# LSH attention and two-layer network on one core: the products of the second layer regrouped by type, and one more raw weight buffer

## The chip, the cores and the metric

The kernel runs on one core of a Trainium2 chip. The metric is the device time of one execution in microseconds (us). The engines are TensorE (PE, with its weight loads shown apart as PEld), VectorE (DVE), ScalarE (ACT), GpSimd (POOL) and SyncE (SP), which here only issues transfers.

## What is computed

Attention over 4 batches of 8 heads, 768 positions and 64 dimensions, in which a query sees only the keys with the same 6-bit hash; then, on the 3072 tokens of 512 values that it gives, a network with a squared ReLU.

```python
q_bits = einsum(q, proj) > 0 ; k_bits = einsum(k, proj) > 0      # 6 bits each
scores = where(q_bucket == k_bucket, q @ k.T / 8, -1e9)
attn = softmax(scores) ; x = attn @ v                            # x: 3072 x 512
h = x @ w_in                                                     # w_in: 512 x 2048
g = s * max(h, 0)**2 + b
out = g @ w_out                                                  # w_out: 2048 x 512
```

## The kernel before, in words

Everything is unrolled, and the order of the work is made by a planner. Each piece of work is added to `Plan` with an engine, a cost in us, what it reads and writes, and a priority; `Plan.order` plays a list schedule with these costs and sorts the pieces by their planned start. Each engine then works through its own list in that order, and a piece on PE that waits holds all that stand behind it.

Attention goes through 96 slots (batch, head, third of the queries: 256 queries). A slot has score products (lines 621 and 622), a row maximum (626), an exponential (627), a normalization on GpSimd (646) and products with the values (686, or 692 and 698). When the last head of a batch is through, `moe` is called for each third of that batch: 256 tokens and 8 steps of two 128-wide slices of the 2048 hidden values, so 96 steps in all. Its PE work has the lowest priority and fills the places that attention leaves. The first batch is gone through in two passes over the hidden values, as its weights are decoded meanwhile.

A step of `moe` (names and lines as in the profile):
- first layer: 24 products with 256 columns of two fp16 planes of x and w_in (lines 794 to 796) into one PSUM bank (5);
- on ScalarE a ReLU out of the bank (804, tile `rb`, one buffer), the square (805), and s and b applied into `ghb`, in 4-byte form (fp32r, two buffers, 806);
- on GpSimd the same in full precision (807) and what `ghb` lost, as bf16, into `glb` (two buffers, 808). The planner counts 0.77 and 1.27 us for these two;
- second layer: 12 products with 512 columns (line 821), for each of two slices and two groups of 128 tokens three of them: z = 0 is `w` with `ghb`, both in 4-byte form; z = 1 is `wl`, the bf16 rest of w_out, with the upper halves of `ghb` read as bf16; z = 2 is `wp`, w_out as bf16, with `glb`. The token groups add up in PSUM banks 6 and 7.

The second layer comes in parts. With HALVES the first part holds z = 0 and z = 1, taken in turn for each slice and token group (eight products, waiting for `ghb`, `w`, `wl`), and the second part z = 2 (four products, waiting for `glb`). The very last step of the kernel takes all three in turn. The planner counts 0.2343 us for z = 0 and 0.2165 for each of the others. The second layer of a step stands behind the first layer of the following step by priority.

Weights come in 32 blocks, decoded by `decode` (lines 362 to 441) while the first 44 slots run: four w_in blocks and four w_out blocks make a group. A block's raw words are loaded from a transfer on ScalarE's queue (line 381) into one of NWR buffers, taken in turn. A w_out block leaves its buffer as soon as it is decoded. The four w_in blocks of a group hold theirs until their common scale is known (one transpose on PE, line 447, which takes its turn with the scales of the values) and they are split into two planes (433 to 438). A second rule lets at most two blocks be loaded ahead of decoding (`PACE`).

Of the kernel before, what the change touches and what calls it, by code (L numbers as in the profile page):

```python
# [168 lines left out]
def lsh_attention_moe(ctx: ExitStack, tc, q, k, v, proj, w_in, w_out, s, b, out):  # L169
# [26 lines left out]
    def f32(ap):  # L196
        return ap.bitcast(F32)

    def top(ap):

        return ap.bitcast(BF16).rearrange("p (n t) -> p n t", t=2)[:, :, 1]
# [8 lines left out]
    def pe(cost, fn, r, w, pr):  # L210
        plan.add(PE, cost, fn, r, w, pr)

    def dve(n, fn, r, w, pr, ns=None):
        plan.add(DVE, ((n + 64) / 960.0 if ns is None else ns), fn, r, w, pr)

    def act(n, fn, r, w, pr, more=0.0, late_=0.0):
        plan.add(ACT, 0.21 + n / 1470.0 + more, fn, r, w, pr, late_)

    def pool(n, fn, r, w, pr, ns=None):
        plan.add(POOL, (0.08 + n / 430.0 if ns is None else ns), fn, r, w, pr)  # L220

    def some(n, fn, r, w, pr, ways, slow=0.0):

        cost = {ACT: 0.21 + n / 1470.0, DVE: (n + 64) / 960.0, POOL: slow or 0.05 + n / 760.0}
        eng = {ACT: nc.scalar, DVE: nc.vector, POOL: nc.gpsimd}
        plan.any([(e, cost[e], lambda e=e: fn(eng[e])) for e in ways], r, w, pr)
# [135 lines left out]
    def decode(u, pr):  # L362
        src, key = dec[u]
        box = {}
        wi = key[0] == "wi"
        tag = f"wr{u % NWR}"

# [398 lines left out]
    def moe(bb, c, g0=0, g1=NF // 4):  # L766
# [15 lines left out]
        for f0 in range(fa, fz, 2):  # L782
            while nd[0] < f0 // 4 * 8 + 6 + f0 % 4:
                yield
            u = nu[0] % 2
            nu[0] += 1
            fill = 1e5 + 100.0 * nu[0]
            for j in range(2):
                hp, fs = bank[:, 5, j * CH:(j + 1) * CH], slice((f0 % 4 + j) * P, (f0 % 4 + j + 1) * P)
                for cc in range(NC_):  # L790
                    def mm(cc=cc, hp=hp, fs=fs, n=f0 // 4):
                        xc = boxes[cc][0]["t"][:, boxes[cc][1]]
                        w = wt[("wi", n, cc)]
                        nc.tensor.matmul(hp, w[:, 0, fs], xc[:, 0, :], start=(cc == 0), stop=False)  # L794
                        nc.tensor.matmul(hp, w[:, 1, fs], xc[:, 0, :], start=False, stop=False)  # L795
                        nc.tensor.matmul(hp, w[:, 0, fs], xc[:, 1, :], start=False, stop=(cc == NC_ - 1))  # L796
                    pe(0.327, mm, [boxes[cc][2], ("wi", f0 // 4, cc, 0), ("wi", f0 // 4, cc, 1)], [("b", 5)], fill)
            r, rk = rb, "r"
            gh, gl, hk, lk = ghb[:, u], glb[:, u], ("gh", u), ("gl", u)
            g4 = f0 // 4  # L800
            ds, dk = dsc[:, bb, g4:g4 + 1], ("ds", bb, g4)
            if c == 0 and f0 % 4 == 0:
                dve(1, lambda g4=g4, ds=ds: nc.vector.tensor_tensor(ds, vsc[:, bb, 1:2], wsc[:, g4, 1:2], ALU.mult), [("sc", bb), ("wsc", g4)], [dk], MP, 0.1)
            some(2 * CH, lambda e, r=r, ds=ds: e.activation(r, bank[:, 5, :], AF.Relu, scale=ds) if e is nc.scalar else e.tensor_scalar(r, bank[:, 5, :], ds, 0.0, ALU.mult, ALU.max), [("b", 5), dk], [rk], MP, (ACT, DVE))  # L804
            act(2 * CH, lambda r=r: nc.scalar.activation(r, r, AF.Square), [], [rk], MP)
            act(2 * CH, lambda r=r, gh=gh: nc.scalar.activation(gh, r, AF.Identity, bias=b_sb, scale=s_sb), [rk, "sb"], [hk], MP, 0.15)  # L806
            pool(2 * CH, lambda r=r: nc.gpsimd.tensor_scalar(r, r, s_sb, b_sb, ALU.mult, ALU.add), [hk, "sb"], [rk], MP, 0.77)  # L807
            pool(2 * CH, lambda r=r, gh=gh, gl=gl: nc.gpsimd.tensor_tensor(gl, r, f32(gh), ALU.subtract), [rk, hk], [lk], MP)  # L808

            end = bb == B - 1 and c == NCH - 1 and f0 == NF - 2  # L810
            for part in ((0, 1), (2,)) if HALVES and not end else ((0, 1, 2),):
                for jt in range(2 * TPC):
                    j, t = (jt % 2, jt // 2) if end else (jt // TPC, jt % TPC)
                    f = f0 + j

                    def mm2(f=f, j=j, t=t, gh=gh, gl=gl, part=part):
                        ts = slice(j * CH + t * P, j * CH + (t + 1) * P)
                        o = bank[:, 6 + t, :]
                        w = wt[("wo", f)]
                        for z in part:  # L820
                            nc.tensor.matmul(o, (gh, top(gh), gl)[z][:, ts], (w[0], w[1], w[2] if PLANE else top(w[0]))[z], start=(f == fa and z == 0), stop=(f == fz - 1 and z == 2))  # L821
                    ks_ = [[hk, ("wo", f, 0)], [("wo", f, 1)], [lk, ("wo", f, 2 if PLANE else 0)]]
                    pe(sum((0.2343, 0.2165, 0.2165)[z] for z in part), mm2, [k for z in part for k in ks_[z]] + [("wo", f, 0)], [("b", 6 + t)], fill + 150)
# [39 lines left out]
    for i in range(NSL):  # L863
        pr = 10.0 * i
        bb, h, c, w = slots[i]
        last = c == NCH - 1
        if last and w + 2 < len(visits):
            parts = prep(w + 2, i, pr)
        if c == h == 0 and bb + 1 < B:
            value_scale(bb + 1, pr + VLATE)  # L870
        weights(i, pr + WP)
        while nd[0] < min(ND, decodes(i)):
            decode(nd[0], pr + 15)
            nd[0] += 1
        now, parts = (parts, []) if not last else (parts[:2], parts[2:])
        values(i, pr + 5, now)
        for bb, h, c, w in [slots[x] for x in closed]:
            last = c == NCH - 1
            if last and w + 2 < len(visits):
                prep_values(w + 2, pr + 12)  # L880
            if h == H - 1:
                todo.append(moe(bb, c, 0, PASS if bb == 0 else NF // 4))
                if bb == 0 and last:
                    todo.extend(moe(bb, c2, PASS, NF // 4) for c2 in range(NCH))
        closed.clear()
        while todo and next(todo[0], True):
            todo.pop(0)
# [14 lines left out]
CONVCOST = 0.95  # L902
RATE = 1.0
PACE = 2
HALVES = True
DSTART = 3
NNAT = 2
NWR = 6
VLATE = 60
VZERO = 10  # L910
TOP = 2.0**15
# [43 lines left out]
```

## Time and profile before

| | us |
|---|---|
| median of 3 runs | 970.77 (969.79 to 971.96) |
| the profiled execution | 973.35 |
| its span, first to last instruction | 971.6 |
| PE busy in the span | 924.2 |
| VectorE, ScalarE, GpSimd busy | 625.5, 660.9, 624.1 |

The profile is of one execution. It gives each instruction's start and duration; matmuls overlap in it, so the cost of one in a row of them is read from the start of one to the start of the next. The granted clock of PE is given as a share of 2.4 GHz. Idle time is put down to what released the engine last; an engine that isn't the bottleneck loses nothing by it.

### The profile page before, as it was taken

To read this page: it belongs to the slowest core of one execution; us is meant where nothing else is said; L and a number is where in the kernel's file an instruction comes from. 1 tells how busy PE (TensorE), PEld (TensorE's weight loads), DVE (VectorE), ACT (ScalarE), POOL (GpSimd) and SP (SyncE) were. 2 spreads that over 40 slices of the span, in tenths; PEclk is the share of its full clock that TensorE was granted. 3 is DMA by queue.
4 is the path that set the end of the run, shared out by engine and by line. 5 is a ranking of instruction groups with operands and counts; after the bars stand their busy time and mean duration, and the time that the engine had idled before them with its cause. 6 is when DMAs were issued, how large, how long until landed. Compare 5 with 4: busy or idle time off the path is not lost.

```text
span 971.6 us, 18091 instructions
## 1 busy us (share of the span) xinstructions
PE 924.2 (95%) x6512; PEld 656.5 (68%) x6512; DVE 625.5 (64%) x1013; ACT 660.9 (68%) x1235; POOL 624.1 (64%) x714
## 2 busy tenths in 40 slices
PE   8999887899988999989999999999999999999997
PEld 5876665666655666757766776777777676666664
DVE  6688897777987676777777867667768775100000
ACT  3788776777767766767777787777687776434342
POOL 2467675768999656657757766676767676443433
PEclk7999989899999999989999999999999999999999
DMA  4376584565886978898899888797797776401000
GB/s 116 92 232 165 148 234 112 166 167 137 230 191 142 193 174 190 196 216 160 152 186 163 175 187 171 155 194 158 164 195 166 152 148 107 109 1 44 11 22 22
DMA packets 303721, 144.44 MB, mean 149 GB/s; under 512 B 264256, under 2 KB 286784, under 8 KB 303632
## 3 DMA queue, kind: packets, MB, share of 16 engines
q1 hardware_dynamic: 298432, 126.25, 60.3%
q10 hardware_dynamic: 5200, 17.05, 5.5%
q8 instruction: 51, 0.84, 0.4%
q14 instruction: 38, 0.31, 0.1%
HBM read 51.38 MB, written 14.16 MB: 67 GB/s over the span
## 4 chain that ended last, share of the span: by engine, by line
PE 56%; POOL 14%; issue 11%; DVE 10%; ACT 6%; DMA 2%; POOLq 0%; SPq 0%; ACTq 0%; DVEq 0%
PE bank L821 15%; PE bank L621 5%; PE bank L794 5%; PE bank L796 5%; PE bank L795 5%; PE bank L622 5%; PE bank L692 4%; POOL glb L808 4%; POOL eb L646 3%; POOL rb L807 3%; DVE st L626 3%; PE bank L686 3%; PE bank L678 3%; PE bank L698 2%; ACT eb L627 2%
## 5 line engine op out<-in xcount | busy, mean ns | idle before, releaser
L646 POOL TENSOR_SCALAR eb<-eb,st 128x768 f32<-128x768 f32 x176 | 194.2, 1110 | 50.3 <-DVE st L637 44.8
L794 PE MATMUL bank<-xc,wi 128*128 128x256 f16 x768 | 211.0, 275 | 1.4 <-ACT rb L804 1.3
L626 DVE TENSOR_REDUCE st<-bank 128x1 f32<-128x768 f32 x192 | 180.2, 952 | 47.0 <-PE bank L622 42.4
L795 PE MATMUL bank<-xc,wi 128*128 128x256 f16 x768 | 210.0, 273 | 0.0
L796 PE MATMUL bank<-xc,wi 128*128 128x256 f16 x768 | 209.9, 273 | 0.0
L627 ACT ACTIVATE eb<-bank,st 128x768 f32<-128x768 f32 x176 | 157.5, 896 | 66.0 <-DVE st L626 33.8
L807 POOL TENSOR_SCALAR rb<-rb,misc 128x512 f32<-128x512 f32 x96 | 84.7, 883 | 166.4 <-ACT ghb L806 164.6
L654 DVE SCALAR_TENSOR_TENSOR pb<-eb,pb 128x768 f16<-128x768 f32 x132 | 146.6, 1123 | 65.3 <-ACT pb L653 63.5
L821 PE MATMUL bank<-w,ghb 128*128 128x512 f32 x384 | 177.4, 534 | 0.0
L621 PE MATMUL bank<-ks,aq 128*128 128x384 f32 x384 | 156.5, 408 | 18.4 <-ACT eb L627 14.5
L804 ACT ACTIVATE rb<-bank,dsc 128x512 f32<-128x512 f32 x95 | 65.2, 687 | 144.2 <-PE bank L796 126.8
L821 PE MATMUL bank<-wl,ghb 128*128 128x512 bf16 x384 | 150.1, 391 | 0.0
L808 POOL TENSOR_TENSOR glb<-rb,ghb 128x512 bf16<-128x512 f32 x96 | 140.8, 1466 | 6.2
L622 PE MATMUL bank<-ks,bq 76*128 76x384 f32 x384 | 133.6, 348 | 1.1 <-DMA bq<-nat 1.1
L653 ACT ACTIVATE pb<-eb 128x768 f16<-128x768 f32 x132 | 108.2, 833 | 15.3 <-DMA tb<-pb 14.2
L821 PE MATMUL bank<-wp,glb 128*128 128x512 bf16 x384 | 102.7, 380 | 4.3 <-POOL glb L808 4.3
L621 PEld LDWEIGHTS bank<-ks,aq 128*128 128x128 f32 x384 | 75.7, 197 | 38.8 <-ACT eb L627 21.3
L821 PEld LDWEIGHTS <-ghb 128*128 128x128 bf16 x384 | 37.2, 97 | 86.6 <-issue 80.5
L794 PEld LDWEIGHTS <-wi 128*128 128x128 f16 x768 | 75.3, 98 | 30.1 <-issue 14.1
L795 PEld LDWEIGHTS <-wi 128*128 128x128 f16 x768 | 75.6, 98 | 19.4 <-issue 2.1
L631 POOL TENSOR_SCALAR st<-st 128x2 f32<-128x2 f32 x96 | 44.3, 462 | 66.5 <-DVE st L626 58.3
L844 DVE COPY osb<-bank 128x256 f32<-128x256 f32 x4 | 1.5, 420 | 127.4 <-PE bank L821 126.8
(141 smaller groups left out, 1656.2 us busy)
## 6 DMA issues: line engine op xcount, KB each, us to landing
ks<-aq SPq DMA_DIRECT2D x60, 192.0 KB
raw<-in_moe_w_in_dram ACTq DMA_DIRECT2D x16, 512.0 KB
raw<-in_moe_w_out_dram ACTq DMA_DIRECT2D x16, 512.0 KB
xc<-xd SPq DMA_DIRECT2D x60, 128.0 KB
nat<-in_q_dram SPq DMA_DIRECT2D x32, 192.0 KB
nat<-in_k_dram SPq DMA_DIRECT2D x32, 192.0 KB
vm<-in_v_dram SPq DMA_DIRECT2D x32, 192.0 KB
xd<-xsb SPq DMA_DIRECT2D x48, 128.0 KB
```

The source lines that it names most:

```text
L621: nc.tensor.matmul(o, aq[:, ts], ks[0][:, cols], start=True, stop=False)
L622: nc.tensor.matmul(o, bq[0:HR, ts], ks[1][0:HR, cols], start=False, stop=True)
L626: dve(S, lambda a=a, sc=sc: nc.vector.tensor_reduce(nm[:, a:a + 1], sc, AX.XY, ALU.max, negate=True), bk, [nk[a]], pr, 0.88)
L627: act(S, lambda a=a, sc=sc, e=e: nc.scalar.activation(e.rearrange("p (g n) -> p g n", g=2), sc, AF.Exp, bias=nm[:, a:a + 1], accum_out=z[: ...
L646: eng.tensor_scalar(e, e, rz[:, a:a + 1], u[:, a:a + 1], ALU.mult, ALU.add)
L654: dve(S, lambda e=e, hi=hi, lo=lo: nc.vector.scalar_tensor_tensor(lo, e, TOP, hi, ALU.mult, ALU.subtract), [ek, hk], [("lo", n)], pr, 1.0)
L794: nc.tensor.matmul(hp, w[:, 0, fs], xc[:, 0, :], start=(cc == 0), stop=False)
L795: nc.tensor.matmul(hp, w[:, 1, fs], xc[:, 0, :], start=False, stop=False)
L796: nc.tensor.matmul(hp, w[:, 0, fs], xc[:, 1, :], start=False, stop=(cc == NC_ - 1))
L807: pool(2 * CH, lambda r=r: nc.gpsimd.tensor_scalar(r, r, s_sb, b_sb, ALU.mult, ALU.add), [hk, "sb"], [rk], MP, 0.77)
L808: pool(2 * CH, lambda r=r, gh=gh, gl=gl: nc.gpsimd.tensor_tensor(gl, r, f32(gh), ALU.subtract), [rk, hk], [lk], MP)
L821: nc.tensor.matmul(o, (gh, top(gh), gl)[z][:, ts], (w[0], w[1], w[2] if PLANE else top(w[0]))[z], start=(f == fa and z == 0), stop=(f == f ...
```

## The change

The second layer's parts are now (z = 0) and (z = 1, z = 2): a step's four 4-byte products come first, waiting for `ghb` and `w`, and then eight bf16 products, waiting for `ghb`, `wl`, `wp` and `glb`. The last step of the kernel keeps all three in turn. NWR goes from 6 to 7: one more buffer of 4 KB a partition for raw weight blocks. The planner orders the whole program anew with both; no instruction is added or removed.

```diff
-            for part in ((0, 1), (2,)) if HALVES and not end else ((0, 1, 2),):
+            for part in PARTS if not end else ((0, 1, 2),):
...
-HALVES = True
+PARTS = ((0,), (1, 2))
...
-NWR = 6
+NWR = 7
```

## Rows read from the trace of the kernel before

**Rows 1.** The page: busy us (share) and instructions; chain that ended last; one group.
```profile
span 971.6 us, 18091 instructions
PE 924.2 (95%) x6512; PEld 656.5 (68%) x6512; DVE 625.5 (64%) x1013; ACT 660.9 (68%) x1235; POOL 624.1 (64%) x714
...
PE 56%; POOL 14%; issue 11%; DVE 10%; ACT 6%; DMA 2%; POOLq 0%; SPq 0%; ACTq 0%; DVEq 0%
...
L821 PE MATMUL bank<-w,ghb 128*128 128x512 f32 x384 | 177.4, 534 | 0.0
```

**Rows 2.** Stretches: length, busy us (instructions) by engine, granted PE clock, DMA share, GB/s.
```profile
250.00:300.00 50.00, 43.50 (x274) 28.62 (x272) 43.39 (x78) 35.09 (x62) 47.98 (x46) 1.00 0.78 183
350.00:415.00 65.00, 64.71 (x448) 45.03 (x447) 44.43 (x68) 46.05 (x82) 41.93 (x48) 1.00 0.87 189
415.00:440.00 25.00, 20.91 (x124) 13.94 (x121) 18.84 (x30) 15.51 (x30) 13.55 (x18) 0.86 0.91 207
440.00:500.00 60.00, 59.80 (x413) 42.29 (x413) 45.59 (x64) 43.05 (x77) 43.19 (x50) 1.00 0.86 161
...
845.00:960.00 115.00, 115.00 (x779) 76.93 (x777) 0.00 (x0) 48.33 (x71) 45.19 (x45) 1.00 0.05 18
```

**Rows 3.** Instruction groups from 440 us on: count, busy us, mean ns, idle before.
```profile
L821 PE MATMUL bank<-w,ghb 128*128 128x512 f32 x288 | 133.6, 539 | 0.0
...
L808 POOL TENSOR_TENSOR glb<-rb,ghb 128x512 bf16<-128x512 f32 x72 | 106.2, 1474 | 5.3
...
L807 POOL TENSOR_SCALAR rb<-rb,misc 128x512 f32<-128x512 f32 x72 | 58.4, 812 | 147.0 <-ACT ghb L806 146.8
```

**Rows 4.** Timeline of PE, one step in the tail: start us, duration us, instruction.
```profile
901.83 0.27 PE L795 MATMUL bank<-xc,wi 128*128 128x256 f16 x1
901.94 0.27 PE L796 MATMUL bank<-xc,wi 128*128 128x256 f16 x1
901.97 0.47 PE L821 MATMUL bank<-w,ghb 128*128 128x512 f32 x1
902.28 0.39 PE L821 MATMUL bank<-wl,ghb 128*128 128x512 bf16 x1
...
903.68 0.39 PE L821 MATMUL bank<-wl,ghb 128*128 128x512 bf16 x1
903.91 1.03 PE L821 MATMUL bank<-wp,glb 128*128 128x512 bf16 x4
904.78 0.27 PE L794 MATMUL bank<-xc,wi 128*128 128x256 f16 x1
```

**Rows 5.** Timeline of the weight loads in the same step.
```profile
902.75 0.10 PEld L821 LDWEIGHTS <-ghb 128*128 128x128 bf16 x1 [0.26 <-issue]
```

**Rows 6.** Timeline of PE where a second layer begins behind attention's 4-byte products.
```profile
729.26 0.39 PE L821 MATMUL bank<-w,ghb 128*128 128x512 f32 x1
729.49 0.39 PE L821 MATMUL bank<-wl,ghb 128*128 128x512 bf16 x1
```

**Rows 7.** Timeline of GpSimd and PE in the tail, the following step.
```profile
905.46 1.26 POOL L808 TENSOR_TENSOR glb<-rb,ghb 128x512 bf16<-128x512 f32 x1
...
907.32 0.47 PE L821 MATMUL bank<-w,ghb 128*128 128x512 f32 x1
```

**Rows 8.** PE's waits, 185 to 440 us (us, times, longest), and one of them.
```profile
PE bank L821 <- POOL glb L808: 2.9, 2, 1.8
...
276.70 1.26 POOL L808 TENSOR_TENSOR glb<-rb,ghb 128x512 bf16<-128x512 f32 x1
...
278.02 0.82 PE L821 MATMUL bank<-wp,glb 128*128 128x512 bf16 x3 [1.12 <-POOL glb L808]
```

**Rows 9.** Weight decoding: two raw loads as issued; VectorE's steps, ns min/median/max.
```profile
72.93 0.34 ACTq L381 DMA_DIRECT2D raw<-in_moe_w_out_dram  x1
...
109.25 0.34 ACTq L381 DMA_DIRECT2D raw<-in_moe_w_out_dram  x1
...
L396 DVE SCALAR_TENSOR_TENSOR raw<-osb,raw x32: 674/691/1540, 58.4 to 305.7; 128x512 int32<-128x512 int32 x32
```

## Prediction

> **What bounds the kernel now.** I read the page first, then the busy times by stretch, then single matmuls in order of time. The page gives TensorE (PE) 95% of the span and no other engine more than 68%, and PE has the largest share of the chain that ended last [rows 1]. A busy PE need not be PE at its peak, so I looked stage by stage [rows 2]. From 440 us on PE has no idle time to speak of (59.80 of 60 us at 440 to 500, 115.00 of 115 at 845 to 960) at the full granted clock, the 2.4 GHz level. Before that it waits: 43.50 of 50 us at 250 to 300, and 20.91 of 25 at 415 to 440, where the granted clock averages 0.86, so it stood at 1.2 GHz for part of the stretch, after waits for work. The reason lies in the order of work: the layers of a batch can start only when its last head is through attention. So there are two regimes. Up to about 440 us attention with its other engines sets the pace and PE time is worth little; from 440 us on the end is set by PE's own work, and each nanosecond taken out of it moves the end by about one.
>
> 72 of the 96 second-layer steps lie behind 440 us: of the 384 four-byte products [rows 1], four to a step, 288 start there [rows 3]. The last step keeps its old order by the code, so 71 count.
>
> **What regrouping the products removes.** One step of the tail shows the cadence, read from start to start [rows 4]. The last first-layer product starts at 901.94, the first bf16 product (wl) at 902.28: 0.34 less the 0.11 that a first-layer product takes (901.83 to 901.94) leaves 0.23 for the four-byte product (w) between them. From there to the fourth wl, 903.68, are three pairs in 1.40 us: 0.467 a pair. The fourth wl takes 0.23 (to 903.91), and the four wp products 0.87 (to 904.78): 0.2175 each. The step's twelve products take 2.73 us.
>
> So a bf16 product costs 0.2175 behind another of its kind, but 0.23 behind a four-byte one; that leaves 0.237 of a pair for a four-byte product behind a bf16 one. The weight loads give the reason for the first: the load for a wl product starts only at 902.75, when that product itself starts, having stood 0.26 us for "issue" [rows 5]; it isn't drawn ahead into the four-byte product.
>
> No 512-column four-byte product follows another in this trace, so the new cost of w is bounded. The nearest row is one that follows a four-byte product of attention, 384 columns wide: from 729.26 to 729.49, 0.23 us [rows 6]. I take 0.23, as it is the same instruction in the same neighbourhood. The lower end is a bf16 product's 0.2175, the upper end the 0.237 that it costs now.
>
> After the change a step has four w (0.23 each), one wl behind a four-byte product (0.23) and seven bf16 products behind bf16 ones (0.2175): 0.92 + 0.23 + 1.52 = 2.67 us, against 2.73: 0.06, or 0.057 with the terms unrounded. With w at 0.237 behind w only the three bf16 products gain, 3 x 0.0125 = 0.0375. With w at 0.2175 everywhere a step would take 2.61 and gain 0.12.
>
> 71 steps x 0.057 = 4.0 us, all in the stretch where PE is saturated (ends: 2.7 and 8.5). The 24 earlier steps save 1.4 us of PE time, but PE waits there and the next batch's start is attention's; between 0 and 1.4 I take 0.5, since only 350 to 415 us is nearly saturated (64.71 of 65) [rows 2].
>
> **What the regrouping adds: an earlier wait.** Four wl products that needed only ghb now stand behind the wait for glb (GpSimd), and behind them everything on PE, which is in order. So eight products need glb at 0.9 us into the step and not four at 1.9. In the tail the glb of a step ends at 905.46 + 1.26 = 906.72 and its first w starts at 907.32 [rows 7]; the first bf16 product would come at 908.24, so 1.5 us of slack cover it (2.5 now). I cost the wait at nothing there; the cover is the first layer of the following step, 24 products of 0.11, that stand ahead of it. If that cover were gone, up to 0.9 us of PE a step would show, the four wl that no longer fill the wait. In the earlier regime PE has waited for glb in two places already, 2.9 us [rows 8]; these may grow by 0.9 each, in a stretch where PE waits anyway. ghb is held until the wl products are done, up to 0.9 us longer; it has two buffers and a step's period is 5.35 us (first w at 901.97 [rows 4], the next step's at 907.32 [rows 7]), so nothing waits for that.
>
> **The seventh raw buffer.** Weight block 6 is loaded at 109.25 us although the one before it was issued at 72.93: the four w_in blocks of a group hold their buffers until their common scale is known [rows 9]. With seven buffers one more w_out block per group can be loaded and decoded ahead of that. It is work moved, not added: its two long VectorE steps (0.69 us each) [rows 9], the ScalarE and GpSimd steps beside them, and its load on ScalarE's queue go from behind the scale to ahead of it, past attention's steps in the same queues. Each moved block can push attention's chain back by up to 1.4 us, or relieve it by as much where the blocks now come in a burst. Two groups of the four have such a long hold in the trace, so the price lies between -2.8 and +2.8 us; I take 0, because total work is the same and its consumers, the steps up to 300 us, are paced by attention. The planner also lays out the whole order anew; the stretch of lowered clock at 415 to 440 (0.86 of 25 us: 7 us at 1.2 GHz, 3.5 us of work lost) [rows 2] can shrink or grow with it. That is the largest single thing which a new order can move.
>
> **The sum.** 4.0 + 0.5 = 4.5 us less. The profiled execution took 973.35 us (span 971.6), so 968.85 for a like one; it lies 2.6 above the median of 970.77, and the same difference makes 966.3 us.
>
> **The rivals.** (a) Order is neutral: a product has its price from its columns and type alone, and 0.237 and 0.23 are noise of the record. Rows 4 speak against it, as 0.2175 and 0.23 are the same kind of product in one step; for it speaks that no run of four w is on record. Then the time stays at 970.8 and only the plan's luck moves it. The Trainium skill, "TensorE: Matmul & The Clock Gate", section "Back-to-back issue gap", gives a gap of N/2.4 + 2.5 ns with no word of type or neighbour; for 512 columns that is 215.8 ns for each of the twelve in either order. The trace agrees for wp (0.2175) and not for w or for a wl behind w.
>
> (b) Half the gain: w costs 0.237 behind w, and the early saving is lost: 2.7 us, 968.1.
>
> (c) The front gains as well: the seventh buffer evens out the decoding and the first layer of the second batch starts earlier, or the low clock at 415 to 440 goes: 3 to 4 us more, about 962.5. For it: VectorE and GpSimd are the busy engines up to 300 us (43.39 and 47.98 of 50) [rows 2]. Against it: no engine's wait for a raw load stands among the waits of the trace.
>
> (d) Slower, by the wait for glb. The planner counts glb's two GpSimd steps at 0.77 and 1.27 us (lines 807 and 808); behind 440 us they take 0.81 and 1.47 [rows 3], 0.25 later. Where the planner puts the eight products right at its own arrival of glb, PE stands 0.25 us. This decides once the slack of 1.5 us is planned away; if that happens in the 48 steps between 440 and 845 us, 48 x 0.25 = 12 us are lost against 4.5 gained: 978.3. One step shows how it looks: glb runs from 276.70 to 277.96, and wp starts at 278.02 after 1.12 us of waiting [rows 8]. Against it: PE has attention and the next first layer to put in between.
>
> **How the numbers follow.** Forecast 0.45 (963.5 to 968.2), (a) 0.14, (b) 0.15, (c) 0.15, (d) 0.11. What a measurement of this kernel can tell from no change is about 0.2%, 1.9 us. Faster by more: the forecast, (c) and most of (b), 0.72; within: (a) and the rest of (b), 0.17; slower: (d), 0.11. The range leaves out (d) and the outer part of (c); it runs from 10.3 us less (the forecast's 4.5 with nearly all of the raw buffer's 2.8 and the clock's 3.5) to 0.7 more (order neutral, a little lost in front): 960.5 to 971.5.
>
> **What would show it.** Right: in the tail four w start 0.23 apart, a step of twelve takes 2.67 and the period of a step falls by 0.06 us; the stretch from the last attention product to the end is 1.4 us shorter. Wrong: the w stand 0.237 or more apart, PE's waits for glb add up to more than 4 us, or the time from which PE is saturated (440 us now) moves by more than 3 us, in which case the front and not the products decided.

## The result, and the profile after

The changed kernel takes 960.28 us (median of 4 runs, 958.97 to 960.83); the kernel before, run beside it, 971.37 (4 runs, 969.79 to 972.27). The ratio is 0.9886, with an interval from 0.9868 to 0.9903: 11.1 us less, where 4.5 were forecast. The direction was right and the time was not: 960.28 lies 0.2 below the range. The profiled execution took 960.04 us.

The page of the changed kernel: span and busy time, then the chain's shares, then two groups.

```profile
span 958.2 us, 18106 instructions
...
PE 914.1 (95%) x6512; PEld 669.1 (70%) x6512; DVE 620.5 (65%) x1004; ACT 660.2 (69%) x1242; POOL 616.8 (64%) x716
...
PE 71%; POOL 10%; issue 9%; DVE 7%; ACT 2%; POOLq 0%; DVEq 0%; ACTq 0%
...
L821 PE MATMUL bank<-wp,glb 128*128 128x512 bf16 x384 | 146.5, 382 | 6.5 <-POOL glb L808 6.5
...
L821 PE MATMUL bank<-w,ghb 128*128 128x512 f32 x384 | 118.2, 415 | 0.0
```

PE's share of the chain rose from 56% to 71% [rows 1]: attention's other engines set less of the end. The busy time by stretch of the changed kernel (length, busy us and instructions of each engine, granted clock, DMA share, GB/s):

```profile
250.00:300.00 50.00, 41.72 (x269) 28.45 (x268) 42.13 (x76) 35.94 (x64) 45.85 (x46) 0.97 0.82 180
350.00:415.00 65.00, 64.84 (x452) 47.12 (x451) 50.90 (x74) 47.12 (x86) 43.73 (x51) 1.00 0.95 200
415.00:440.00 25.00, 22.47 (x147) 15.27 (x147) 19.70 (x28) 17.49 (x31) 16.73 (x23) 1.00 0.95 209
440.00:500.00 60.00, 60.00 (x431) 44.31 (x430) 43.87 (x62) 44.65 (x81) 39.19 (x46) 1.00 0.89 169
845.00:950.00 105.00, 105.00 (x714) 73.47 (x711) 0.00 (x0) 44.52 (x64) 39.98 (x40) 1.00 0.05 18
```

Against [rows 2], PE has done more at 415 to 440 (147 products, not 124) and the granted clock there is 1.00, not 0.86. From 440 us on PE is saturated in both.

To see where the time went I took three marks that both traces have: the `glb` step (line 808) of the first step of the second batch and of the last step before the final batch, and the last product. First the kernel before:

```profile
441.06 1.27 POOL L808 TENSOR_TENSOR glb<-rb,ghb 128x512 bf16<-128x512 f32 x1
...
833.46 1.28 POOL L808 TENSOR_TENSOR glb<-rb,ghb 128x512 bf16<-128x512 f32 x1
...
967.65 0.38 PE L821 MATMUL bank<-wp,glb 128*128 128x512 bf16 x1
```

Then the changed one:

```profile
434.40 1.88 POOL L808 TENSOR_TENSOR glb<-rb,ghb 128x512 bf16<-128x512 f32 x1
...
821.03 1.29 POOL L808 TENSOR_TENSOR glb<-rb,ghb 128x512 bf16<-128x512 f32 x1
...
954.01 0.38 PE L821 MATMUL bank<-wp,glb 128*128 128x512 bf16 x1
```

The front, up to the first mark, gave 6.7 us; the stretch between the marks went from 392.4 to 386.6, 5.8 less; the tail from 134.2 to 133.0, 1.2 less. The three add up to 13.6 us, 2.5 more than the medians give, as the profiled execution of the kernel before is one of its longer ones (973.35 us, 2.0 above the median of 971.37) and that of the changed kernel isn't (960.04 for 960.28). Of the front's 6.7, 0.7 stand already at PE's 300th product, where both kernels still have the same order of products. Even so, about half of the gain lies where the prediction had put 0.5.

### The profile page after: what moved, and what is told of

It reads as the page before. It is cut to its first block, busy times and chain, and to the rows that moved or that the text cites. A ratio compares the mean times of both kernels' runs of the same rounds, so it can differ in the third digit from the quotient of the medians.

```text
span 958.2 us, 18106 instructions
## 1 busy us (share of the span) xinstructions
PE 914.1 (95%) x6512; PEld 669.1 (70%) x6512; DVE 620.5 (65%) x1004; ACT 660.2 (69%) x1242; POOL 616.8 (64%) x716
## 4 chain that ended last, share of the span: by engine, by line
PE 71%; POOL 10%; issue 9%; DVE 7%; ACT 2%; POOLq 0%; DVEq 0%; ACTq 0%
PE bank L821 20%; PE bank L621 7%; PE bank L794 7%; PE bank L795 6%; PE bank L796 6%; PE bank L622 6%; PE bank L692 5%; PE bank L678 3%; PE bank L686 3%; POOL glb L808 3%; PE bank L698 3%; DVE st L626 2%; POOL eb L646 2%; POOL rb L807 2%; PE bank L491 2%
## 5 line engine op out<-in xcount | busy, mean ns | idle before, releaser
L646 POOL TENSOR_SCALAR eb<-eb,st 128x768 f32<-128x768 f32 x176 | 196.4, 1122 | 53.7 <-DVE st L637 42.3
L654 DVE SCALAR_TENSOR_TENSOR pb<-eb,pb 128x768 f16<-128x768 f32 x132 | 148.8, 1134 | 52.1 <-ACT pb L653 51.0
L621 PE MATMUL bank<-ks,aq 128*128 128x384 f32 x384 | 151.6, 395 | 10.8 <-ACT eb L627 7.1
L821 PE MATMUL bank<-wp,glb 128*128 128x512 bf16 x384 | 146.5, 382 | 6.5 <-POOL glb L808 6.5
L821 PE MATMUL bank<-wl,ghb 128*128 128x512 bf16 x384 | 147.7, 385 | 0.0
L808 POOL TENSOR_TENSOR glb<-rb,ghb 128x512 bf16<-128x512 f32 x96 | 135.8, 1415 | 6.1
L821 PE MATMUL bank<-w,ghb 128*128 128x512 f32 x384 | 118.2, 415 | 0.0
L794 PEld LDWEIGHTS <-wi 128*128 128x128 f16 x768 | 75.2, 98 | 34.6 <-issue 18.3
L795 PEld LDWEIGHTS <-wi 128*128 128x128 f16 x768 | 75.5, 98 | 19.7 <-issue 3.2
L796 PEld LDWEIGHTS <-wi 128*128 128x128 f16 x768 | 75.2, 98 | 8.8
```

The source lines that it names most:

```text
L621: nc.tensor.matmul(o, aq[:, ts], ks[0][:, cols], start=True, stop=False)
L646: eng.tensor_scalar(e, e, rz[:, a:a + 1], u[:, a:a + 1], ALU.mult, ALU.add)
L654: dve(S, lambda e=e, hi=hi, lo=lo: nc.vector.scalar_tensor_tensor(lo, e, TOP, hi, ALU.mult, ALU.subtract), [ek, hk], [("lo", n)], pr, 1.0)
```

## The experiments

Each run is compared with the kernel before, run beside it on the same chip. "Count" is the planner's cost of a second layer's four-byte product, 0.2343 us in both kernels. Changing it changes nothing that is computed, only the plan: the order of the pieces and, for some copies and elementwise steps, which engine takes them, as the planner picks that too. PE's products stay the same 6512. On the other engines a new plan shifts the counts a little, as with the count 0.2283:

```profile
PE 921.7 (96%) x6512; PEld 656.5 (68%) x6512; DVE 620.1 (64%) x1009; ACT 667.0 (69%) x1247; POOL 612.1 (63%) x704
```

Before, they are 1013, 1235 and 714 [rows 1], and in the changed kernel 1004, 1242 and 716: that no instruction is added or removed holds for PE. "Order" stands below for both, the order and these engines.

**One part at a time.** One kernel has the new parts with six buffers, the other the old parts with seven.

```diff
-            for part in ((0, 1), (2,)) if HALVES and not end else ((0, 1, 2),):
+            for part in PARTS if not end else ((0, 1, 2),):
-HALVES = True
+PARTS = ((0,), (1, 2))
```

> The regrouped parts with six raw buffers as before. If the products alone make the gain, 960.3 us and the second batch's first layer starts 7 us earlier here too. If the seventh buffer makes the gain up to there, 5 to 6 us less than before (about 966), with the first 440 us unmoved.

```diff
-NWR = 6
+NWR = 7
```

> The parts of before with seven raw buffers. If the buffer makes the gain up to the second batch's start, 6 to 7 us less than before (about 964.5) with the tail's step at 5.35 us as before. If the buffer is worth nothing, 971 us, within 2 us.

Measured: 963.76 us for the parts alone (ratio 0.9918, 0.9903 to 0.9933) and 962.62 for the buffer alone (0.9904, 0.9884 to 0.9924). Each gives most of the whole gain, so they don't add up: 0.9918 x 0.9904 would be 0.9823, and the two together gave 0.9886. The buffer alone removes no product and changes no group, and yet its first mark lies at 430.7 and its end at 956.3. In both, the planner has laid out the program anew. The next two runs take that apart.

**The regrouping without a new order.** The planned order of the kernel before is kept; where products of one second-layer step stand next to each other on PE, their four-byte products are emitted first, then the wl and then the wp (the change takes wl and wp in turn).

```diff
+                    if not end:
+                        mine[len(plan.steps)] = (nu[0], part, mm2)
...
-            plan.steps[i][0][0][2]()
+            if i not in run:
+                plan.steps[i][0][0][2]()
+            elif i == run[i][-1]:
+                for x in run[i]:
+                    if 0 in mine[x][1]:
+                        mine[x][2](only=(0,))
+                for x in run[i]:
+                    mine[x][2](only=tuple(z for z in mine[x][1] if z))
```

> The order planned for before, engine by engine; only where second-layer products of one step stand next to each other on PE are the four-byte ones put first. Cadence alone: the tail's step goes from 5.347 to about 5.293 us, and 71 such steps give 3.9 us less (967.5); a step with attention in between gains less. If regrouping also frees attention's chain, more than 6 us less. If the gain was the new order's, under 1 us less.

**A new order without the regrouping.** The kernel before, with another count.

```diff
-                    pe(sum((0.2343, 0.2165, 0.2165)[z] for z in part), mm2, ...
+                    pe(sum((0.2373, 0.2165, 0.2165)[z] for z in part), mm2, ...
```

> The kernel before, but the planner counts a four-byte product at 0.2373 us and not 0.2343: no instruction changes, the order does from the first step of the layers (about 155 us) on. If a new order by itself moves the time by several us, this differs from 971.4 by more than 2 us either way; if orders are all alike, it is within 1 us.

Measured: 969.37 for the regrouping in the old order (0.9974, 0.9963 to 0.9985), which is 2.5 us less (1.5 to 3.6). For the new order alone 966.46 (0.9944, 0.9921 to 0.9968): 5.4 us less without a change to any product or piece of work.

The timeline of PE in the tail of the kernel regrouped in the old order:

```profile
891.54 0.27 PE L796 MATMUL bank<-xc,wi 128*128 128x256 f16 x1
891.57 1.18 PE L821 MATMUL bank<-w,ghb 128*128 128x512 f32 x4
892.58 1.04 PE L821 MATMUL bank<-wl,ghb 128*128 128x512 bf16 x4
893.46 1.03 PE L821 MATMUL bank<-wp,glb 128*128 128x512 bf16 x4
894.32 0.27 PE L794 MATMUL bank<-xc,wi 128*128 128x256 f16 x1
```

From 891.54 to 894.32 are 2.78; less 0.11 for the first-layer product the twelve take 2.67, as the prediction worked out. In this trace the marks lie at 439.36 and 828.96 and the last product at 961.97: 2.8 less between the marks and 1.2 less behind them, 4.0 together. The front's 1.7 is no gain of the regrouping: this execution is 2.2 us ahead already at PE's 300th product (49.07, where the profile of before has 51.31), so that counted from there its front is 0.5 longer. And the low clock stays where it was:

```profile
415.00:440.00 25.00, 20.49 (x125) 13.81 (x123) 18.55 (x29) 15.66 (x29) 12.55 (x19) 0.86 0.95 209
```

So the products' own gain in the trace is the size that was forecast, and something else moved the front. The candidates were the low clock, the seventh buffer, and the luck of the planner's order.

**Is it the low clock?** The order of before, with PE filled at the place where the clock falls: extra products behind each attention step of PE between the third and the fourth group of products of the second batch's first step (44 products with two fillers, 22 with one). They multiply by zeros and add nothing to the bank.

```diff
+    none = tile_("none", [P, P], F16)
+    nc.vector.memset(none, 0.0)
...
+                        lots[0] = lambda hp=bank[:, 5, 0:CH]: nc.tensor.matmul(hp, none, ..., start=False, stop=False)
...
             plan.steps[i][0][0][2]()
+            if open_ and n >= 1 and plan.steps[i][0][0][0] == PE and i not in mine:
+                for _ in range(FILLERS):
+                    lots[0]()
```

> The order of before, with two more 256-column products (stationary operand zero, so nothing is added) behind each attention step on PE from the third product group of the second batch's first step to its fourth: 44 products of 0.11 us in the stretch of 415 to 434 us where PE waits. If the low clock of 430 to 436 us comes of these waits and costs time, it is gone and the time is 1.5 to 3.4 us less than before. If the added work only delays attention, 0 to 3 us more.

> The same with one added product for each step, 22 in all. If half the filling is enough, the clock stays at 2.4 GHz here too and the time is 2 to 3.4 us less; if it isn't, the time is that of before.

The same stretch with two fillers:

```profile
415.00:440.00 25.00, 22.99 (x171) 15.81 (x169) 19.11 (x30) 16.27 (x30) 13.73 (x19) 1.00 0.94 199
```

and with one:

```profile
415.00:440.00 25.00, 22.30 (x154) 14.80 (x153) 20.48 (x32) 17.65 (x33) 15.87 (x20) 1.00 0.97 211
```

The fillers of the first of the two, from its instruction groups at 415 to 440 us (count, busy us, mean ns, idle before; four of the 44 lie ahead of 415):

```profile
L801 PE MATMUL bank<-xc,none 128*128 128x256 f16 x40 | 7.8, 277 | 0.0
```

The granted clock is 1.00 where it was 0.86, and the time is 972.0 and 972.1 us: ratio 1.0008 for both (0.9991 to 1.0024, and to 1.0025). The low clock is gone and nothing is won. The added products could in principle cost what the clock gave back; but the second filler adds 22 of them, 2.4 us of PE's time, and moves nothing. A gain of more than 0.9 us from the clock alone isn't in the intervals, so it isn't what the new orders win by.

**Is it the buffer, or the order?** The four combinations of parts and buffers, at two more counts.

> The kernel before with the four-byte product counted at 0.2313 us by the planner: another order of the same instructions. If the order of before is an unlucky draw, this too is 4 to 8 us below it (964 to 968). If the draw of the other changed count was the lucky one, it stays at 970 to 974.

> Seven raw buffers, parts of before, four-byte product counted at 0.2373 us: a second order for the seventh buffer alone. If the buffer itself is worth 4 us or more, 959 to 964, below the same count with six buffers (966.5). If the buffer's gain was its order's, 965 to 970.

> Regrouped parts, six raw buffers, count 0.2373: a second order for the parts alone. With 3 to 4 us from the cadence and the rest from the order, 962.5 to 966; if the parts' own effect on the order is what counts, 960 to 963.

> The changed kernel with the count at 0.2373: a second order for both edits. If both edits have effects of their own that add up, 958 to 962; if the order decides, anywhere from 958 to 968.

> Seven raw buffers, parts of before, planner's count 0.2313 us: third order for the buffer alone. If the buffer is worth about 4 us whatever the order, near 967.5 (971.7 with six at this count). If it is worth nothing of itself, 970 to 974.

> Regrouped parts, six raw buffers, count 0.2313: third order for the parts alone. With about 3.5 us of the parts' own, near 968; if their gain came with the order, 970 to 974.

> Both edits, count 0.2313: third order. If 3.5 us of the parts and 4 us of the buffer add up, near 964; if the orders decide, anywhere from 960 to 972.

Then five buffers, and the old parts with six and seven buffers at two further counts:

> The kernel before with five raw buffers in place of six. If buffers for raw blocks are worth about 4 us each, some 4 us or more slower than before (975 and up) with the decoding done later; if only orders differ, 964 to 973.

> Six raw buffers, parts of before, planner's count 0.2403 us: a fourth order of the same instructions. From the three so far (ratios 1, 0.9944, 1.0011) anywhere from 965 to 973.

> Seven raw buffers, parts of before, count 0.2403. If the buffer is worth 3 to 4 us on the average of the orders, the mean of this and the next such pair lies that much below the six-buffer ones (this one 960 to 969); if nothing, no such difference.

> Six raw buffers, parts of before, planner's count 0.2283 us: a fifth order of the same instructions, 965 to 973 by the spread so far.

> Seven raw buffers, parts of before, count 0.2283. With an own effect of the buffer of 3 to 4 us, 962 to 968; without one, as with six buffers.

Measured, as ratios to the kernel before (the intervals are 0.0012 to 0.0031 to each side; the medians run from 960.28 to 975.56 us):

| count | old parts, 6 buffers | old parts, 7 | new parts, 6 | new parts, 7 |
|---|---|---|---|---|
| 0.2283 | 0.9960 | 0.9988 | | |
| 0.2313 | 1.0011 | 0.9936 | 0.9943 | 0.9954 |
| 0.2343 | 1 (before) | 0.9904 | 0.9918 | 0.9886 (after) |
| 0.2373 | 0.9944 | 0.9978 | 0.9974 | 0.9932 |
| 0.2403 | 1.0046 | 0.9976 | | |

Five buffers with the old parts at 0.2343 gave 0.9997 (0.9978 to 1.0017).

The first column is the main finding. Five orders of the same work, with the same buffers, take 966.31, 971.7, 971.37, 966.46 and 975.56 us: 9 us from the best to the worst, twice what was forecast for the whole change. The kernel before stands in the middle of them (their mean is 0.9992). The changed kernel is the fastest of all that were run, and 0.0038 (3.7 us) below the mean of its own column, 0.9924, which has three orders.

The parts: over the three counts that all four columns have, the new ones are lower by 0.0040 with six buffers (0.9985 to 0.9945) and by 0.0015 with seven (0.9939 to 0.9924); the mean, 0.0028, is 2.7 us. With three orders a column it is a rough figure (a standard error of 1.8 us from the six differences), but it is in line with the 2.5 of the regrouping in the old order. The buffer: over five counts the old parts have a mean of 0.9992 with six and 0.9956 with seven, 3.5 us apart, with a standard error of 2.3 from the spread of the orders. From the lowest count to the highest it is +2.7, -7.3, -9.3, +3.3 and -6.8 us, of either sign, and five buffers are no slower than six at the same count. What the buffer is worth by itself stays open.

One order shows how such luck looks. The slowest kernel (count 0.2403, six buffers) has the full clock at 415 to 440, and PE is busier there than before:

```profile
415.00:440.00 25.00, 24.49 (x165) 16.94 (x163) 19.49 (x29) 16.81 (x32) 17.34 (x22) 1.00 0.91 199
```

Yet it takes 4 us more than the kernel before. Its marks lie at 437.22 and 827.66 and its last product at 970.58: 3.8 us are won in the front and 2.0 between the marks, and 8.7 lost in the tail. PE's waits from 815 us on tell most of it (us in total, times, longest):

```profile
PE bank L794 <- DMA xc<-xd: 5.4, 1, 5.4
```

and its timeline of PE has the place:

```profile
838.58 0.37 PE L794 MATMUL bank<-xc,wi 128*128 128x256 f16 x1 [5.41 <-DMA xc<-xd]
```

The first layer of the final batch waits for the transfer of x; this order puts no other work on PE ahead of it, and some of attention's products stand behind it. After the wait the granted clock is at its low level of 1.2 GHz:

```profile
838.50:842.50 4.00, 3.92 (x23) 2.58 (x24) 0.00 (x0) 0.47 (x1) 0.00 (x0) 0.52 0.37 66
```

The first 15 products there start 0.213 apart and not 0.109, 1.6 us more, and as PE is saturated nothing gives that back. In the trace of before, PE has no such wait. The order with count 0.2283 and six buffers is the opposite case. At 415 to 440 it has less done and a lower clock than before,

```profile
415.00:440.00 25.00, 18.95 (x114) 13.74 (x112) 16.00 (x27) 15.37 (x28) 13.42 (x14) 0.80 0.95 191
```

and it is 4 us faster.

## Why the prediction was wrong

**What bounds the kernel: right.** PE is saturated from 440 us on in both traces, and what left its work there left the time.

**The regrouping's 4.0 us: right in mechanism, and in size by the trace; 2.5 by the medians.** The tail of the changed kernel, PE's timeline:

```profile
894.16 0.27 PE L796 MATMUL bank<-xc,wi 128*128 128x256 f16 x1
894.19 1.18 PE L821 MATMUL bank<-w,ghb 128*128 128x512 f32 x4
895.21 0.39 PE L821 MATMUL bank<-wl,ghb 128*128 128x512 bf16 x1
895.43 0.38 PE L821 MATMUL bank<-wp,glb 128*128 128x512 bf16 x1
895.65 0.38 PE L821 MATMUL bank<-wl,ghb 128*128 128x512 bf16 x1
...
896.73 0.38 PE L821 MATMUL bank<-wp,glb 128*128 128x512 bf16 x1
896.95 0.27 PE L794 MATMUL bank<-xc,wi 128*128 128x256 f16 x1
```

The timeline runs equal instructions together; in shorter stretches it has the starts of the second, third and fourth w:

```profile
894.51 0.86 PE L821 MATMUL bank<-w,ghb 128*128 128x512 f32 x3
...
894.74 0.62 PE L821 MATMUL bank<-w,ghb 128*128 128x512 f32 x2
...
894.97 0.40 PE L821 MATMUL bank<-w,ghb 128*128 128x512 f32 x1
```

The w stand 0.23 apart, as forecast; the last takes 0.24 to the first wl, and seven steps of bf16 products, from 895.43 to 896.95, take 1.52 (0.217 each). The twelve take 2.68 (896.95 - 894.16 - 0.11), against 2.67 forecast and 2.73 before [rows 4]. The period of a step fell from 5.347 to 5.293, by 0.054. From the last attention product to the last product are 129.8 us before, and 128.6 in the changed kernel as well as in the one regrouped in the old order: 1.1 less, where 1.4 was named. In that order the sum came out at 4.0 by the traces behind the first mark and 2.5 (1.5 to 3.6) by the medians, so 4.0 lies a little above what the chip gives; the 0.5 that this trace's front is longer, counted from a like start, would make it 3.5.

The load of the first bf16 weights still isn't drawn ahead into a four-byte product; with four in a row that is paid once a step and not four times:

```profile
895.20 0.10 PEld L821 LDWEIGHTS <-ghb 128*128 128x128 bf16 x1 [0.27 <-issue]
895.22 0.10 PEld L821 LDWEIGHTS <-glb 128*128 128x128 bf16 x1
895.44 0.10 PEld L821 LDWEIGHTS <-ghb 128*128 128x128 bf16 x1
```

Behind it the loads start 0.21 ahead of their products (895.22 for 895.43).

The whole stretch between the marks can be accounted for in the same way. I give each product its start-to-start time among its own kind (0.230 for w, 0.216 for wl and wp, 0.178 and 0.1745 for attention's four-byte ones, 0.109 to 0.110 with 256 columns, 0.052 at line 698), and count what lies above that, by unbroken runs of four-byte products:

| us between the marks | before | regrouped, old order | after |
|---|---|---|---|
| products at their own price | 377.0 | 377.0 | 375.9 |
| above it, at runs of four-byte products | 8.55 in 252 runs | 5.64 in 138 | 4.37 in 126 |
| above it, elsewhere | 6.91 | 6.96 | 6.38 |
| sum | 392.5 | 389.6 | 386.7 |

A run of w costs about 0.02 us whether it has one product or four (the median of the 160 single w of before, and 1.05 - 0.109 - 0.92 = 0.02 for the four above); the table's sums hold stalls beside that. Of the 5.8 us, 2.9 are the regrouping's. The other 2.9 came with the new order: 1.1 of work that lies outside the marks now (6 of attention's products and 6 of the first layer's), 1.3 of stalls and changes of type among attention's runs, 0.6 elsewhere.

**The wait for glb at nothing: right in the tail, a little low in front.** In the tail:

```profile
892.39 1.27 POOL L808 TENSOR_TENSOR glb<-rb,ghb 128x512 bf16<-128x512 f32 x1
```

It ends at 893.66, 1.55 us before the first wl; 1.5 was forecast. PE's waits at 185 to 440 us:

```profile
PE bank L821 <- POOL glb L808: 5.1, 2, 3.5
...
PE bank L621 <- ACT eb L627: 1.9, 2, 1.8
```

and behind 440 us:

```profile
PE bank L821 <- POOL glb L808: 1.4, 1, 1.4
```

Two waits of 2.9 [rows 8] became two of 5.1: 2.2 more, where up to 1.8 was named. The one behind 440 is the kernel's last step and is 1.4 before as well. The bar that I had set, 4 us in all, was no test: with that last step the kernel before already has 4.3.

**The front: the step that failed.** I priced the seventh buffer at 0 within 2.8 and the early saving at 0.5, and let the new order only shrink or grow the low clock's 3.5. The sign that I had named for this error came: the time from which the second batch runs moved by 6.7 us (6.0 from a like start). What the buffer does was right (the block that was loaded at 109.25 [rows 9] is loaded at 76.60), but its price can't be told from the order's:

```profile
76.60 0.34 ACTq L381 DMA_DIRECT2D raw<-in_moe_w_out_dram  x1
```

The error is in taking the front as given and giving the new order no term of its own. Nor is it the front alone: the other 2.9 us between the marks, where PE is saturated, came with the order too. A new order is a draw from a spread of some 9 us (a standard deviation of 0.0041, 4 us, in the first column), and any edit to the planner's input makes a new draw, the change of a count by 1% too. With such a term, of both signs, the range would have been some us wider at either end and the time inside it. Of the 11.1 us, 2.5 to 4.0 are the products'; the 3.7 by which the changed kernel lies below the mean of its column's three orders is the draw, as far as three orders tell; the rest is the buffer or the draw, and the runs can't part them. What in the order shortened the front isn't shown. One difference is that attention on PE waits less for the exponential: 1.9 us in the rows above, and before at the same place:

```profile
PE bank L621 <- ACT eb L627: 7.5, 8, 1.5
```

**The low clock as the largest thing an order can move: wrong.** The fillers took it away for nothing (1.0008), one order had a lower clock there and was 4 us faster, and another had the full clock there and was the slowest. That one has other low stretches at 272 to 300 us (0.82 on average) and still reaches its first mark 3.8 us ahead of before; its low clock behind the wait in the tail, where PE is saturated, did cost 1.6. At 415 to 440 PE waits for attention, and the likely reason, which no run tests by itself, is that work done faster there waits for the same thing a little later.

**The rivals.** (a) falls: order isn't neutral, as the kernel regrouped in the old order shows. The rule of the Trainium skill, "TensorE: Matmul & The Clock Gate", section "Back-to-back issue gap", which that section gives for an isolated product, comes to an estimated 215.8 ns for each of the twelve in either order; the trace agrees for bf16 behind bf16 (0.216) and not for w behind w (0.230). (b) falls, as w behind w is 0.23. (d) falls: behind 440 us PE waits for glb no longer than before. (c), that the front gains as well, is nearest, though neither of its two reasons is shown: the clock isn't it, and the buffer's part is open.

**What stays open.** What the seventh buffer is worth over many orders, and why one order's front is shorter than another's: the first mark lies anywhere from 427.8 to 441.1 us in the 16 kernels of the table (the starts of the profiled executions alone, up to the 300th product, differ by up to 3.0 us), and an early one isn't all gain (427.8 with the new parts, seven buffers and count 0.2313 ends at 966.9 us, as 395.4 lie between its marks, where the changed kernel has 386.6).

## What to carry to other kernels

Where PE is saturated, read the price of a product from start to start by its type and by what stands before it, and put products of one type together: each run of four-byte products among bf16 or fp16 ones cost 0.02 us here, whether it had one product or four. Where a planner sets the order, an edit is two changes, itself and a new draw: freeze the order to measure the first, move a cost by a per cent to see the spread of the second, and credit the edit only with what is left over several orders. Follow a stall or a low clock to the end before pricing it: the one at 415 to 440 was removed and gave nothing, and a wait with a low clock behind it in the saturated tail of another order cost 7.0 us (5.4 and 1.6).

## What the runs showed of the hardware

A 512-column four-byte product takes 0.230 us behind its own kind, and about 0.24 where a bf16 product follows; a bf16 one takes 0.216 to 0.217 behind its own kind and 0.22 to 0.23 right behind a four-byte one (895.21 to 895.43 above, 903.68 to 903.91 in [rows 4]). The first bf16 weight load behind a four-byte product stands 0.26 to 0.27 us for issue, whether one or four such products came before. The granted clock returned to 1.00 at 415 to 440 with the extra products placed in PE's gaps; this moved no time. At a granted clock of 0.52, the 1.2 GHz level, behind a wait of 5.4 us, 256-column products start 0.213 us apart and not 0.109.
